# Where the copied sums of the second sweep's seven-product groups are added: in VectorE's accumulators, or by DMA in device memory

## The chip, the cores and the metric

The kernel runs on one core of a Trainium2 chip. The metric is the device time of one execution in microseconds (us), and the median of several runs is compared.

## What is computed

The reference takes attention over 32 memory slots per head, then a leaky two-layer network, then a bilinear one. The change touches the last of the three, and in it the last product alone:

```python
n_tokens, d_model, d_ff = (2304, 512, 1536)
...
def _moe2_ref(x, w_a, w_b, w_out) -> np.ndarray:
    a = x @ w_a
    b = x @ w_b
    return (a * b @ w_out).astype(np.float32)
```

## The kernel before

Activations stand with features on the 128 partitions and tokens along the columns; the result `out` lies in device memory as 128 partitions x 4 feature blocks x 2304 tokens. Every f32 operand is split into a high and a low part, and a product is three matrix passes of 512 columns each.

The bilinear stage runs in two **sweeps** over the hidden features (s = 0 and s = 1), each over half of the tokens; s = 1 is the last thing that the kernel does. A sweep takes the 1536 hidden features in 12 pieces of 128 (c = 0 to 11), two pieces forming a group q = 0 to 5. For each piece `ab_unit` (L1061) makes `a * b`, and for each group the product with `w_out` is added to the sweep's accumulators.

For q = 0 to 4 of the second sweep that last product is made in Strassen's manner, with seven products for a 2 x 2 split instead of eight: `o_part` issues one of them for a row half x (x = 0, 1), three passes at L1277. Four accumulators in SBUF, named `osum` and numbered d = 2, 3, 4, 7, hold the four quarters of the result. Products number 1, 6 and 7 are running sums in PSUM; ScalarE copies each to an SBUF tile `ok` (L1297). Products 2, 5 and 3 end a sum that VectorE adds from PSUM to `osum` 2, 7 and 3 (L1311, one SBUF and one PSUM input), and the copy `ok` belongs there too: in q = 0 VectorE makes `osum` of both at once (L1309), and in q = 1 to 4 it adds `ok` to `osum` by an instruction of its own (L1314, both inputs in SBUF). `osum` 4 has no copy to add.

The sixth group (q = 5) has eight plain products, made by `o_unit` (L1158, six passes each) at the very end, when nothing else is left for TensorE. VectorE adds each from PSUM to `osum` (L1171), and SyncE then issues the DMA of that part to `out` (L1179): twelve transfers, in the order in which the parts are finished. The last product is cut into a piece of 320 and one of 192 columns, so that the last addition and the last transfer are short.

The order of all instructions on each engine is written out by hand in two tables: `ORDER` lists the operations by number, with a letter for the engine where there is a choice, and `PLACES` gives every tile its room. SBUF tiles share 29 rooms named s0 to s28; a tile that takes over a room waits until the last reader of the tile before it is done. Each engine runs its own list in order, and an instruction that waits holds up all behind it on that engine.

Of the kernel before, what the change touches and what calls it, by code (L numbers as in the profile page):

```python
# [12 lines left out]
ALU = mybir.AluOpType  # L13
# [4 lines left out]
P = 128  # L18
# [10 lines left out]
NB2 = 512  # L29
# [55 lines left out]
def c_dma(nbytes):  # L85
    return max(0.6, nbytes / DMA_RATE)
# [7 lines left out]
305v 344 266a 168 103 141 267 268a 338 142 306a 127 345 269 337 143v 104 167 128 154 144 106 340 339a 145 155 342 108a 129 156 130 146v 158 131 343a 118 341
147 160a 119 364 121a 120a 132v 169 148a 105 86v 133 157 319 122 149v 318 134 153 260 320v 358 261a 123a 262 310 135v 263a 309 264 136 170 311v 124 151 172a
384 126v 137a 372 125a 138v 365a 107 312 159 390 179 109a 385 313 386 171 321 161a 391 110 314v 173a 373 322 359a 354 152 111a 323v 374 392 112 375v 348
113a 114v 315a 352 324a 316v 356 325v 355 349 387v 350 180 351v 393v 370 357v 298v 307v 181 360 97v 371a 353a 182 366 362 361 183 376 368 367 363v 184v 369v
185 174 377a 186 270 541 382 273a 271a 175a 272 187v 394 383a 274 188 176 532 346 178a 189a 177a 190v 395a 378 505 191 379 380 162 193 347a 192 194 275 550
195v 559 396 276a 278a 277 196 279 388 163a 197 542 414 381v 389a 198v 406 415 199 416 398 544v 200a 417v 164 201v 418 165a 166a 397 543 399v 545 407a 213
533 546 412 215 547v 214 548a 216 202 552 534 402 203 204 419a 217v 413a 408 561 205 403 280 409 206v 218 424 404 281a 405v 410 411v 432 425a 219 283a 436  # L100
434 207 282 208 285 437a 560 284 426 209v 433 288a 430 428 289 507 210 427 286a 211a 287 400 220v 431a 551 212v 420 221 442 429v 498 222a 535v 484 421 223v
491 422 423v 450 443a 435v 506 536 438 562v 451 537 452 444 401a 563 458 553v 446 453v 439 448 440 564 445 459 554 460 538v 441v 462 565v 447v 466 463 555
464 566a 454 556v 467 461v 472 468 455 456 478 557a 457v 567v 539a 470 499 549v 1274 492 1300 540v 1281 473 558v 479 449a 465v 474 469v 485 476 475v 486
508v 480 471a 481v 493 509 501v 500 494v 482 510 477a 1275 502 503 495 487v 496 572 483a 488 1276 489 1301 497v 1302 511v 490v 578 573a 504v 1277v 1303v 512
1278 579a 1304 1279 584 513a 515a 514 1305 590 1280v 516 1292a 1306v 585a 568 1293v 1307 1308a 1282 574 1310 1309v 1283 1284v 1314 522 569 1285 570 1286 575
580 576 1287v 591a 571v 586 581 1288v 1294a 577v 596 582 1289v 587 583v 588 1290v 1296a 1291v 589v 592 1298a 1297v 525a 598 593 1312 523a 602 1315 594 1322
595v 1341 1295v 1299v 604 524 1313 610 605 1311 526 606 608 597a 603 607v 517 609 614 520a 518a 521 1316 519 612 620 611 600 613v 599 601v 615 622 744 1318v
621 616 1319 624 623 626 617 1317 634 618 627 619v 630 1342 1320 628 625v 527 631 629v 632 1321v 644 765 633v 1333v 751 654 792 645 758 636 646 635 530a
528a 1343 529 638 1323 637v 1324 648 531 639 1334v 640 1344v 1351 1325v 647v 1345 641v 650 1326 649 656 651 652 662 653v 1346 660 801 663 1327 657 664 1328v
658 1347v 1335a 655 1348 1349a 668 1329v 746 1331v 1330v 642 1350v 1337a 1336v 1332v 753 661 745 1338v 752 674 665v 1353 759 1352 672 1339a 810 760 1355  # L110
1340v 643 1354 666 659v 675 670 676 669 677v 767 678 667 766 754v 671v 802 747v 793 761v 684 748 794 768v 679 804v 673 680 755 819 795v 690 682 762 811 796
685 681 803 769 813v 686 812 805 814 692 687 691 688 696 689v 694 693 749 756 770 702 820 683v 821 806 797 710 763 704 712 695v 1382 711 698 708 1356 699
700 1363 705 701v 706 697 822v 714 815 718 703 716 715 823 722 707v 719 717v 720 713v 726 723 721v 724 750v 730 727 757v 728 824 709 764v 771v 738 725v 798v
772 731 799a 729v 736 807v 816v 808a 800v 775a 740 825v 732 776 826a 809v 832 733 827v 773a 817a 774 739 734 741v 1357 818v 840 1358 735v 1364 1359v 828 833
1365 737 1384 834 1366v 1383 1360 742 842 1361 1362v 1385v 850 841 743 836 1374v 835 830 829 1367 856 851 837v 843v 1386 858 857 846 844 848 847 849v 831v
838 845 1368 864 839 782 852 783a 862 784 853 859 1369v 854 1375v 1376a 855v 860 777 1392 785a 1370v 1387 868 780a 863 1388v 778a 1371v 1389 1390v 870 1373v
874 786 871 865 866 861v 1378a 1372v 1391v 872 880 1380a 779 1396 1397 781 867v 876 1379v 873v 886 1394 877 1377v 878 1423 882 1381v 1404 890 881 1395 883
884 1393 787 885v 891 892 879v 887 869 888 894 1004 788a 889v 1011 893v 790a 898 875 1018 789 904 791 908 905 906 899 907v 900 895 1398 896 916 1405 897v
1400v 1399 1061 910 1401 1424 901v 1402 914 1025 1052 1403v 1407v 1415a 911 1416v 912 1406 1426v 902 1433 1408 918 913v 1425 1409 917 909 1427 1428 920
1429v 1410v 919v 915 928 1070 922 930 1431a 932 929 1432v 924 1006 903 1437 1013 1430 921 926 923 1411v 1005 1412v 1020 1414v 1413v 1417a 934 925v 1012  # L120
1419v 938 1026 931v 1019 1007v 935 936 944 1027 939 927 1053 937v 1054 1021v 962 1014v 1028v 933 1008 1009 940 1029 1071 952 1022 1015 1063 1055v 950 941
945 1062 1023 942 1064v 1072 1030 946 953 954 943v 958 1016 956 1073v 1079 960 1056 947 1065 959 1421a 1066 948 970 949v 951 964 955v 1074 974 1010v 965 966
968 971 963 975 961v 972 1017v 976 1031v 982 1057 969 986 984 1024v 978 957 973v 1032 1075 979 983 967v 980 998 988 981v 977v 1058v 992 1067v 990 1059v 993
999 1000 985v 994 1076v 1068a 1060v 1035a 1077a 996 991 1033a 987 1069v 1080 1036 1081 995v 1001v 1002 1078v 1420v 1034 1435 1438 1422v 1418v 1436 1092 997
1434 1445 1003 1464 989v 1082v 1083 1094 1084 1093 1088 1085v 1440 1042 1096 1095 1086a 1100 1439 1087v 1098 1043a 1089 1044 1090 1045a 1091v 1112 1101 1046
1102 1447 1110 1441v 1103v 1446 1097v 1442 1443 1106 1444v 1104 1108 1099 1107 1448v 1456a 1109v 1466 1111 1116 1457v 1113 1465 1449 1474 1114 1450 1122
1105 1467v 1115v 1451v 1118 1452v 1123 1124 1454v 1119 1453v 1120 1128 1458a 1117 1468 1126 1455v 1462a 1130 1125 1129 1121v 1176 1132 1127v 1460a 1037 1131
1461v 1528v 1476 1134 1038a 1040a 1039 1177 1041 1178 1047 1133v 1529v 1136 1459v 1135 1142 1137 1463v 1138 1146 1050a 1469 1477 1143 1150 1475 1144 1179v
1147 1145v 1148 1154 1470v 1139v 1472a 1140 1149v 1151 1051 1505 1152 1048a 1471 1155 1479 1049 1158 1156 1486 1153v 1141 1164 1160 1473v 1159 1162 1157v
# [164 lines left out]
def tile_mem_attention__leaky_mlp__bilinear_mlp(  # L294
# [842 lines left out]
    def o_unit(s, c, l, e, pos, cols=None):  # L1137
# [303 lines left out]
```

## Time and profile before

| | us |
|---|---|
| median of 3 runs | 778.22 |
| lowest, highest | 776.81, 778.3 |
| span of the profiled execution, from its first to its last instruction | 775.6 |
| TensorE busy in that span | 767.0 |
| VectorE busy | 647.7 |
| ScalarE busy | 402.6 |
| GpSimd busy | 0.7 |

The profiled execution is listed by its span. The median of the runs is 2.6 us longer than this span; that is what lies around it. TensorE's granted clock is 0.993 of its full level of 2.4 GHz over the span. GpSimd's 0.7 us all lie in the first two microseconds; it issues no DMA. All 59808 packets of the kernel's own data go through one queue, which SyncE feeds.

### The profile page before, as it was taken

Reading aid. Unit: us, or ns where it says so; the run is one execution under the profiler, and the core shown is the slowest. Engines: PE = TensorE matmul, PEld = TensorE weight load, DVE = VectorE, ACT = ScalarE, POOL = GpSimd, SP = SyncE. Lnnn points to the kernel's source line nnn. Section 1 sums busy time; section 2 is a strip of 40 time slices with the busy share of each in tenths; the row PEclk is TensorE's granted clock in tenths of the full one; section 3 lists DMA queues with packets and bytes.
Section 4 is the critical chain, followed back from the end, with each engine's and each line's share of the span. In section 5 each row is a group of like instructions: output and inputs, shape, how many; then the busy total and the mean of one; then the engine's idle time right before and its main releaser. Section 6 shows DMA issues by size and latency. Waiting matters only on the chain.

```text
span 775.6 us, 12742 instructions
## 1 busy us (share of the span) xinstructions
PE 767.0 (99%) x4766; PEld 656.8 (85%) x4766; DVE 647.7 (84%) x1249; ACT 402.6 (52%) x866; POOL 0.7 (0%) x6
## 2 busy tenths in 40 slices
PE   7999999999999999999999999999999999999998
PEld 6577898899889978898988888888888888888886
DVE  5897899689877989698685789999999688789877
ACT  5685786675546646654433445644543424444330
POOL 0000000000000000000000000000000000000000
PEclk9799999999999999999999999999999999999999
DMA  9993241665039141635973629775798685765523
GB/s 321 374 323 109 84 164 68 200 235 177 1 129 331 58 144 74 245 109 216 375 268 118 219 82 332 263 256 199 235 339 326 241 314 171 253 244 202 182 105 108
DMA packets 59868, 158.89 MB, mean 205 GB/s; under 512 B 7520, under 2 KB 22880, under 8 KB 59808
## 3 DMA queue, kind: packets, MB, share of 16 engines
q1 hardware_dynamic: 59808, 158.09, 57.6%
q8 instruction: 37, 0.61, 0.3%
q14 instruction: 23, 0.19, 0.1%
HBM read 111.41 MB, written 46.66 MB: 204 GB/s over the span
## 4 chain that ended last, share of the span: by engine, by line
PE 96%; DMA 2%; SPq 0%; DVE 0%; ACT 0%; issue 0%
PE y L840 24%; PE abx L1061 17%; PE h L788 13%; PE abz L1061 8%; PE o L1158 6%; PE os_x L1277 6%; PE aby L1061 4%; PE os_z L1277 3%; PE a L1115 2%; PE b L1115 2%; PE y L836 2%; PE vw L719 2%; PE os_y L1277 2%; DMA phi<-in_phiT_dram 1%; PE km L562 1%; DMA raw_win<-in_w_in_dram 1%
## 5 line engine op out<-in xcount | busy, mean ns | idle before, releaser
L840 PE MATMUL y<-g,wout 128*128 128x320 f32 (+2 forms) x1104 | 198.3, 333 | 0.0
L840 PEld LDWEIGHTS y<-g,wout 128*128 128x128 f32 x1104 | 175.0, 188 | 18.0 <-issue 3.8
L1061 PE MATMUL abx<-yb_T,wo 128*128 128x512 f32 x432 | 110.0, 390 | 0.0
L1061 PEld LDWEIGHTS abx<-yb_T,wo 128*128 128x128 f32 x432 | 80.1, 188 | 16.8 <-ACT t L1072 0.6
L1072 ACT COPY t<-abx 128x512 f32<-128x512 f32 x72 | 42.0, 586 | 61.7 <-PE abx L1061 60.6
L788 PE MATMUL h<-ahi,vwh 128*128 128x320 f32 (+1 forms) x240 | 72.8, 303 | 0.0
L788 PE MATMUL h<-ahi,vwl 128*128 128x320 f32 (+1 forms) x240 | 71.0, 296 | 0.0
L788 PE MATMUL h<-alo,vwh 128*128 128x320 f32 (+1 forms) x240 | 71.0, 296 | 0.0
L804 DVE TENSOR_TENSOR g<-t,g 128x256 fp32r<-128x256 f32 (+1 forms) x120 | 52.6, 452 | 15.9 <-ACT t L741 11.8
L741 ACT ACTIVATE g<-h 128x320 fp32r<-128x320 f32 (+1 forms) x120 | 48.3, 416 | 33.4 <-PE h L788 30.6
L741 ACT ACTIVATE t<-h 128x256 f32<-128x256 f32 (+1 forms) x120 | 49.4, 419 | 26.2 <-PE h L788 24.9
L1297 ACT COPY ok<-os_x 128x512 f32<-128x512 f32 x54 | 31.7, 586 | 58.9 <-PE os_x L1277 52.8
L788 PEld LDWEIGHTS h<-ahi,vwh 128*128 128x128 f32 x240 | 45.4, 189 | 8.0 <-issue 5.0
L859 DVE TENSOR_TENSOR acc<-y,acc 128x320 f32<-128x320 f32 (+1 forms) x72 | 39.3, 552 | 9.7 <-PE y L840 9.5
L788 PEld LDWEIGHTS h<-alo,vwh 128*128 128x128 f32 x240 | 45.5, 189 | 0.6
L788 PEld LDWEIGHTS h<-ahi,vwl 128*128 128x128 f32 x240 | 45.5, 190 | 0.0
L1069 DVE TENSOR_TENSOR t<-abz,t 128x512 f32<-128x512 f32 x48 | 32.9, 685 | 8.7 <-PE abz L1061 5.9
L1061 PE MATMUL abz<-yb_B,wo 128*128 128x512 f32 x144 | 36.7, 390 | 0.0
L1061 PE MATMUL abz<-yb_T,wo 128*128 128x512 f32 x144 | 36.6, 390 | 0.0
L1061 PE MATMUL abx<-yb_B,wo 128*128 128x512 f32 x144 | 36.5, 390 | 0.0
L1061 PE MATMUL aby<-yb_B,wo 128*128 128x512 f32 x144 | 36.5, 390 | 0.0
L1158 PE MATMUL o<-p,wout 128*128 128x512 f32 (+2 forms) x150 | 35.6, 383 | 0.0
(372 smaller groups left out, 1447.6 us busy)
## 6 DMA issues: line engine op xcount, KB each, us to landing
k_wo<-wo SPq DMA_DIRECT2D x24, 512.0 KB, 4.0
wo<-k_wo SPq DMA_DIRECT2D x24, 512.0 KB, 4.6
raw_wout<-in_w_out_dram SPq DMA_DIRECT2D x22, 512.0 KB, 5.4
raw_win<-in_w_in_dram SPq DMA_DIRECT2D x16, 512.0 KB, 6.6
kv<-in_kv_dram SPq DMA_DIRECT2D x16, 512.0 KB, 10.2
wf<-k_wf SPq DMA_DIRECT2D x9, 512.0 KB, 4.4
k_yb_T<-yb_T SPq DMA_DIRECT2D x8, 512.0 KB, 6.3
yb_T<-k_yb_T SPq DMA_DIRECT2D x8, 512.0 KB, 5.8
```

The lines of the kernel that those rows point to most:

```text
L741: nc.scalar.activation(dst, src, AF.Prelu, alpha=0.01)
L788: nc.tensor.matmul(T[o], T[w[u]][:, k, fs], T[a[v]][:, k, cols], start=(k == 0 and i == 0), stop=(k == 1 and i == 2))
L804: lambda T, e: engines[e].tensor_tensor(T[g][:, i, 1, to], T[t], T[g][:, i, 0, to].bitcast(F32), op=ALU.subtract),
L840: nc.tensor.matmul(T[o], w[:, u, here], T[g][:, j, v, at:at + m], start=(f == 0 and p == 0), stop=(f == 3 and p == 2))
L859: "DVE", c_dve(m), lambda T: nc.vector.tensor_tensor(T[acc][:, i, :], T[o], T[acc][:, i, :], op=ALU.add),
L1061: nc.tensor.matmul(T[o], T[w][:, which, u, k * P:(k + 1) * P], T[ys[v]][:, k, :], start=first and k == 0 and x == 0, stop=k == 1 and x == ...
L1069: op("DVE", 0.69, lambda T: nc.vector.tensor_tensor(T[to], T[o], T[x], op=ALU.add), r=[o, x], w=[to], tiles=[o, x, to])
L1072: op("ACT", 0.59, lambda T: nc.scalar.copy(T[t], T[X]), r=[X], w=[t], tiles=[X, t])
L1115: nc.tensor.matmul(T[o], T[w][:, k // 2, u, k % 2 * P:(k % 2 + 1) * P], T[ys[v]][:, k, :], start=(k == 0 and x == 0), stop=(k == 3 and x = ...
L1158: nc.tensor.matmul(T[o], T[w][:, u, es], T[g][:, at, v, here], start=(x == 0 and k == 0), stop=(x == 1 and k == 2))
L1277: nc.tensor.matmul(T[o], lhs(T, u), T[g][:, v, :], start=i in (1, 2, 5) and k == 0, stop=k == 2, skip_group_check=True)
L1297: op("ACT", 0.59, lambda T: nc.scalar.copy(T[k][:, x, :], T[o]), r=[o], w=[(k, x)], tiles=[o, k])
```

## The change

In the second sweep, for q = 1 to 4, VectorE's addition of `ok` to `osum` (L1314) goes away. In its place GpSimd issues DMAs from `ok` to the result in device memory: for q = 1 they write, for q = 2 to 4 they carry `accum_op` and add to what stands there. A copy of `osum` 2 is one transfer of 512 columns; one of `osum` 3 or 7 is two, of 320 and 192 columns. At the end the parts of `osum` 2, 3 and 7 can no longer overwrite `out`, so their DMAs move from SyncE to GpSimd and add as well; those of `osum` 4 stay on SyncE as they were. The first sweep is as before. The two tables are rewritten because the operations have new numbers.

```diff
@@ o_unit
+                d = acc[1] if s else 0
+                more = [("out", d, i, at)] if s and d != 4 else []
                 op(
-                    "DMA", c_dma(P * w * 4), lambda T, at=at, w=w, to=to: nc.sync.dma_start(out[:, e, to:to + w], T[acc][:, i, at:at + w]),
-                    r=[(ka, base) if cols else ka], tiles=[acc], ahead=1e12,
+                    "DMA", c_dma(P * w * 4),
+                    lambda T, at=at, w=w, to=to, more=more: (nc.gpsimd if more else nc.sync).dma_start(
+                        out[:, e, to:to + w], T[acc][:, i, at:at + w], **({"accum_op": ALU.add} if more else {})
+                    ),
+                    r=[(ka, base) if cols else ka], w=more, tiles=[acc], ahead=1e12,
                 )
@@ o_part
         if m:
-            op(
-                two(NB2), 0, lambda T, e: engines[e].tensor_tensor(into(T), into(T), T[k][:, x, :], op=ALU.add),
-                r=[(k, x)], w=[tok(d)], tiles=[k, acc(d)], ahead=1e12, soon=True,
-            )
+            hh, l = PART[d]
+            if s:
+                for at, w_, to in places_of(s, l):
+                    op(
+                        "DMA", 0,
+                        lambda T, at=at, w_=w_, to=to: nc.gpsimd.dma_start(
+                            out[:, 2 * hh + x, to:to + w_], T[k][:, x, at:at + w_], **({"accum_op": ALU.add} if q > 1 else {})
+                        ),
+                        r=[(k, x)], w=[("out", d, x, at)], tiles=[k], ahead=1e12, soon=True,
+                    )
+            else:
...
```

TensorE's and ScalarE's lists hold the same operations in the same order in both kernels. VectorE's list lacks 24 rows, SyncE's lacks 10, and GpSimd's has 50 more.

At the end of the kernel before, SyncE's list holds the transfers of the finished accumulators. In the names, `osum_3` is accumulator d = 3, `out_0_dram` is the result, and the brackets name the semaphores on which the instruction waits:

```order
L1179 DMA out_0_dram<-osum_3_7357 128x192 [waits DMAHW5_49,DVE_49]
L1179 DMA out_0_dram<-osum_3_7357 128x320 [waits DMAHW6_49]
L1179 DMA out_0_dram<-osum_2_7262 128x512 [waits DMAHW7_49]
L1179 DMA out_0_dram<-osum_3_7357 128x320 [waits DMAHW0_49,DVE_49]
L1179 DMA out_0_dram<-osum_3_7357 128x192 [waits DMAHW1_49]
L1179 DMA out_0_dram<-osum_7_7313 128x320 [waits DMAHW2_49,DVE_49]
L1179 DMA out_0_dram<-osum_7_7313 128x192 [waits DMAHW3_49]
L1179 DMA out_0_dram<-osum_7_7313 128x320 [waits DMAHW4_49,DVE_49]
L1179 DMA out_0_dram<-osum_7_7313 128x192 [waits DMAHW5_49,DVE_49]
```

The same nine transfers are GpSimd's last nine rows in the changed kernel:

```order
L1184 DMA out_0_dram<-osum_3_7357 128x192 [waits DMASW1_49,DVE_49]
L1184 DMA out_0_dram<-osum_3_7357 128x320 [waits DMASW2_49]
L1184 DMA out_0_dram<-osum_2_7262 128x512 [waits DMASW3_49]
L1184 DMA out_0_dram<-osum_3_7357 128x320 [waits DMASW5_49,DMASW4_49,DVE_49]
L1184 DMA out_0_dram<-osum_3_7357 128x192
L1184 DMA out_0_dram<-osum_7_7313 128x320 [waits DMASW6_49,DVE_49]
L1184 DMA out_0_dram<-osum_7_7313 128x192 [waits DMASW7_49]
L1184 DMA out_0_dram<-osum_7_7313 128x320 [waits DMASW0_49,DVE_49]
L1184 DMA out_0_dram<-osum_7_7313 128x192 [waits DMASW1_49,DVE_49]
```

All nine moved, in the same order, from SyncE's list to GpSimd's, behind the 40 transfers of `ok` and one more of `osum_2`. A wait for DMASW with a number is one for the eighth transfer before it on GpSimd's queue.

In the middle of the sweep, at the start of group q = 2, VectorE's list before reads so. Here `ok_1_1_1` is the copy of product 1 of group q = 1, `w2s_1_2` holds the sums of weights of group q = 2 and takes over a room, and `pT` and `pf` are sums of the hidden features:

```order
L1311 TENSOR_TENSOR osum_2_7262<-os_1_1_1_y_7590,osum_2_7262 128x512 [waits PE_49]
L1239 TENSOR_TENSOR pb_1_2_T2_7601<-pT_1_2_7495,pb_1_2_T2_7601 128x512 [waits Activation_49]
L1314 TENSOR_TENSOR osum_2_7262<-osum_2_7262,ok_1_1_1_7478 128x512 [waits DVE_49]
L1229 TENSOR_TENSOR pf_1_5_7542<-pf_1_5_7542,pT_1_2_7495 128x512
L1204 TENSOR_TENSOR w2s_1_2_7620<-wf_1_2_7530 128x256 [waits DMAHW4_49,DVE_49]
```

In the changed kernel it is:

```order
L1318 TENSOR_TENSOR osum_2_7262<-os_1_1_1_y_7593,osum_2_7262 128x512 [waits PE_49]
L1246 TENSOR_TENSOR pb_1_2_T2_7606<-pT_1_2_7498,pb_1_2_T2_7606 128x512 [waits Activation_49]
L1236 TENSOR_TENSOR pf_1_5_7545<-pf_1_5_7545,pT_1_2_7498 128x512
L1211 TENSOR_TENSOR w2s_1_2_7626<-wf_1_2_7533 128x256 [waits DMAHW4_49,DMASW5_49,DMASW0_49]
```

The addition of `ok_1_1_1` is gone, and the instruction that takes over that tile's room waits for GpSimd's transfers out of it instead of for VectorE.

## Rows read from the trace of the kernel before

**Rows 1.** The page: its span, and TensorE's busy time and instructions.
```profile
span 775.6 us, 12742 instructions
PE 767.0 (99%) x4766; PEld 656.8 (85%) x4766; DVE 647.7 (84%) x1249; ACT 402.6 (52%) x866; POOL 0.7 (0%) x6
```

**Rows 2.** Busy time of each engine by stretch, from the first L1314 group on.
```profile
core 0: us, PE busy (x) PEld busy (x) DVE busy (x) ACT busy (x) POOL busy (x), PEclk, DMA share, GB/s
660.00:685.00 25.00, 25.00 (x112) 20.67 (x112) 20.75 (x35) 12.31 (x22) 0.00 (x0) 1.00 0.61 206
685.00:710.00 25.00, 25.00 (x112) 20.71 (x111) 22.36 (x40) 10.22 (x18) 0.00 (x0) 1.00 0.58 213
710.00:735.00 25.00, 25.00 (x112) 20.71 (x111) 20.50 (x36) 9.49 (x18) 0.00 (x0) 1.00 0.68 250
735.00:760.00 25.00, 25.00 (x112) 20.70 (x111) 20.36 (x35) 8.23 (x15) 0.00 (x0) 1.00 0.23 85
760.00:776.00 16.00, 12.54 (x60) 10.34 (x58) 10.73 (x18) 0.62 (x1) 0.00 (x0) 0.98 0.37 131
```

**Rows 3.** The chain that ended last, its end: start, length, engine and line.
```profile
761.32 11.24 PE o L1158 x54
...
772.58 0.36 DVE osum L1171
```

**Rows 4.** VectorE's last instructions in time order: start us, length us, line, idle before.
```profile
768.15 0.69 DVE L1171 TENSOR_TENSOR osum<-o,osum 128x512 f32<-128x512 f32 x1
769.51 0.69 DVE L1171 TENSOR_TENSOR osum<-o,osum 128x512 f32<-128x512 f32 x1 [0.67 <-PE o L1158]
770.87 0.69 DVE L1171 TENSOR_TENSOR osum<-o,osum 128x512 f32<-128x512 f32 x1 [0.67 <-PE o L1158]
771.75 0.49 DVE L1171 TENSOR_TENSOR osum<-o,osum 128x320 f32<-128x320 f32 x1 [0.18 <-PE o L1158]
772.58 0.36 DVE L1171 TENSOR_TENSOR osum<-o,osum 128x192 f32<-128x192 f32 x1 [0.34 <-PE o L1158]
```

**Rows 5.** SyncE's issues at the end, merged and the last alone: start us, length us.
```profile
768.87 3.53 SPq L1179 DMA_DIRECT2D out_dram<-osum  x7
...
773.00 0.38 SPq L1179 DMA_DIRECT2D out_dram<-osum  x1
```

**Rows 6.** Line L1314 between 660 and 776: duration in ns, first and last start.
```profile
L1314 DVE TENSOR_TENSOR osum<-osum,ok x24: 681/684/687, 669.4 to 767.4; 128x512 f32<-128x512 f32 x24
```

**Rows 7.** Line L1179: how long SyncE needs for one issue, ns min/median/max.
```profile
L1179 SPq DMA_DIRECT2D out_dram<-oaccl x16: 332/432/936, 642.3 to 660.9; - x16
L1179 SPq DMA_DIRECT2D out_dram<-osum x12: 332/390/447, 763.4 to 773.0; - x12
```

**Rows 8.** DMA between 763 and 776: rate in 40 slices; issues, KB, us to landing.
```profile
GB/s 0 0 0 44 372 366 25 0 0 0 0 0 246 403 158 0 208 365 233 0 95 208 288 349 391 359 358 314 63 331 304 172 331 300 173 0 0 0 0 0
...
out_dram<-osum SPq DMA_DIRECT2D x4, 256.0 KB, 2.0
...
out_dram<-osum SPq DMA_DIRECT2D x4, 96.0 KB, 1.7
```

**Rows 9.** DMA issues between 660 and 760, the commonest load: KB, us to landing.
```profile
wo<-k_wo SPq DMA_DIRECT2D x21, 512.0 KB, 4.5
```

**Rows 10.** ScalarE's copy of a tile, and VectorE's first instruction in its room.
```profile
672.27 0.59 ACT L1297 COPY ok<-os_x 128x512 f32<-128x512 f32 x1 [1.77 <-PE os_x L1277]
...
678.09 0.42 DVE L1204 TENSOR_TENSOR w2s<-wf 128x256 f32<-128x256 f32 x1
```

More of the change, by code (lines that the diff above doesn't have):

```diff
@@ L94 @@
[L94 to L105, printed above, removed]
@@ L186 @@
[L186 to L188 removed]
+24 246 0 4 238 1 26 25 224 27 3 28 2 247 29 31 30 231 248 249v 34a 250 32a 251 35 33 45 239 240 241v 23 252v 242 253 5 44 243 6 244v 22 36 7 8 46 226 37
@@ new lines @@
+1850v 2024 1858v 1936 1930 2119 2047 2064 1928 1970 1932a 2026 1977v 2039 2025 1994 1999 1971v 2145 1931v 2126 1978a 1972v 2046 2028 1974v 1934a 1973v
+1938a 1975v 2027 2018 1980a 1935v 2040 1981v 2006 1979v 1996 1916 1933v 1982a 2030 1939 2000 1983v 1940a 2008 1997 2065 2002 1995 1941v 2066 2041v 2020a
+2029 2001 2003 2042 2043 2031 2032 2048v 2049 2004 2050 2067v 2044v 2034 2005 2033 2056a 2120 2057v 2009 2121 2051v 2074 2068 2058a 2036 2069 2146 2007
+2147 2086 2035 2128 2010 2127 2059v 2011 2037 2070v 2100 2148v 2071 2072a 2149 2075 2014a 2012 2079 2073v 2015v 2078 2019 2013v 2150 2102 2052v 2053v 2054v
@@ new lines @@
+2151v 2217 2095 2060a 2152 2153a 2061v 2080 2094 2103 2076 2016a 2224 2055v 2101 2062a 2082 2017v 2096a 2063v 2021 2081 2154v 2022a 2083 2088 2106 2023v
+2243 2122v 2084 2325 2129v 2123 2077 2107 2159 2130 2104 2124 2085 2110 2105 2131 2089 2125v 2087 2137a 2108 2132v 2219 2091 2138v 2139a 2109 2218 2155
+2097 2299 2112 2225 2090 2092 2114a 2226 2167 2113 2098a 2111 2133v 2181 2099v 2134v 2093v 2183 2140v 2135v 2156 2136v 2182 2160 2141a 2143a 2142v 2227v
+2185 2157 2161 2220v 2184 2144v 2162 2228 2158 2245 2186 2244 2163 2221 2300 2222 2229 2189 2223v 2230v 2235a 2187 2169 2164 2326 2236v 2327 2165 2231v
@@ new lines @@
+2253 2188 2190 2191 2166 2232v 2233v 2301 2234v 2237a 2168 2170 2239a 2328v 2240v 2193 2246v 2255 2247 2192 2172 2248 2194 2258 2241a 2173 2171 2176 2242v
+2210a 2115v 2256 2302v 2175 2174v 2306 2329 2249v 2281 2177a 2303 2250 2215a 2330 2273 2259 2331v 2251a 2304 2332 2333a 2279 2414 2178 2260 2334v 2305v
+2282 2317a 2261 2280 2179a 2238v 2275a 2318v 2254 2285 2262 2116v 2283 2252v 2263 2211v 2307 2195 2335 2284 2204v 2401 2265 2400 2286 2205a 2257 2309v
+2117a 2180v 2339 2347 2310 2308 2206v 2264 2311 2340 2266 2312v 2270 2267 2319a 2313v 2341 2314v 2355 2196v 2321a 2207v 2197v 2315v 2268 2404 2322v 2316v
@@ new lines @@
+2320v 2287 2271 2274 2288 2198v 2323a 2199v 2269 2405 2208a 2289 2402 2276 2200a 2342 2290 2324v 2371 2212v 2415 2201v 2343 2372 2209v 2294a 2376 2407
+2202a 2292 2203v 2377 2356 2118v 2403 2293 2416 2213a 2272v 2409 2291v 2344 2434 2406 2357a 2214v 2361 2435 2216v 2345 2277a 2295v 2362 2349 2436 2278v
+2296v 2346 2363 2437 2297a 2350 2408 2348 2364 2352 2358 2298v 2359a 2351 2373 2417 2353 2410 2365 2374 2412 2419 2413 2366 2354v 2368 2367v 2398a 2421
+2393v 2420 2369 2438 2394v 2422 2387v 2360v 2439 2444 2423 2440v 2388a 2441 2445 2378 2389v 2424 2375v 2442 2411 2446 2425 2466 2395v 2426 2337 2447 2396a
@@ new lines @@
+2467 2399v 2524 2427 2338 2450 2390v 2448 2443v 2431 2468 2451 2370v 2526 2428 2391a 2488 2449 2429 2397v 2392v 2489 2471 2469 2432 2379v 2486 2381v 2472
+2433v 2509 2487 2380v 2478 2430 2525 2383a 2336 2461a 2384v 2510 2473 2591 2462v 2527 2382v 2480 2385a 2474 2490v 2386v 2491 2492 2475 2463v 2529 2493
+2464a 2465v 2476 2530 2548 2477 2494 2479 2549 2481 2495 2483 2482 2517a 2531 2592 2518v 2496 2532 2497 2484 2498 2499 2485v 2533 2550 2511v 2522a 2534
+2500 2551 2512a 2514v 2501v 2552 2535 2519v 2504 2515a 2503 2502 2553 2520a 2536 2505 2554 2537 2544 2506v 2555 2538 2507 2539 2508 2556 2418 2545 2470
@@ L222 @@
+b7 b1 b2 t1 t4 t0 g1 b3 g7 b4 g4 f7 b4 b4 s12 g6 f0 s10 s22 s10 s18 g3 f1 g0 b0 b6 b5 t2 t3 t1 s6 b3 b3 b4 s3 b3 f1 s13 s23 f1 g3 s2 g1 s4 s13 s11 s9 s11
+b1 b2 b7 t0 t4 t2 s9 f7 g4 b3 b4 b3 f0 g6 s17 s20 s12 s8 f4 g7 s4 s22 b1 b5 b0 t1 t3 t0 s16 b3 b4 s8 b3 f4 g4 s9 s2 s8 g0 f7 s4 g7 s3 s10 s13 s7 s10 b2 b7
+b5 t2 t3 t1 s7 b3 b4 b3 s11 g1 s9 s2 f0 s18 s6 g3 s3 s12 b0 b7 b1 t4 t0 t2 f1 s7 b3 b4 g6 b3 s18 s16 s17 s13 s23 s20 s6 b5 b7 b1 t1 t2 t3 s25 s17 b3 b4 b3
+b3 b4 b3 b4 b3 b4 b3 b4 b3 b4
 """
@@ L1312, in o_part @@
         if m:
-            op(
-                two(NB2), 0, lambda T, e: engines[e].tensor_tensor(into(T), into(T), T[k][:, x, :], op=ALU.add),
-                r=[(k, x)], w=[tok(d)], tiles=[k, acc(d)], ahead=1e12, soon=True,
-            )
+            hh, l = PART[d]
[9 more added lines that the diff above has]
+            else:
+                op(
+                    two(NB2), 0, lambda T, e: engines[e].tensor_tensor(into(T), into(T), T[k][:, x, :], op=ALU.add),
+                    r=[(k, x)], w=[tok(d)], tiles=[k, acc(d)], ahead=1e12, soon=True,
+                )
         if 2 * q + 2 == NC2:
```

223 lines of the change are left out of this document (106 added, 117 removed).

## The prediction

> **What bounds the kernel now.** I read the page first: TensorE is busy for 767.0 of 775.6 us [rows 1]. A busy share of 99% can still hide stalls, so the next view was the table by stretch, over the part that the change touches. In all four stretches from 660 to 760 TensorE is busy for 25.00 of 25.00 us at full clock, while VectorE is busy for 20 to 22 us of each [rows 2]. The reader is to see that TensorE has no gap there that a freer VectorE could close. TensorE's list of operations is the same before and after, so the middle of the sweep can only stay as long as it is or grow.
>
> The other place is the end. The chain that ended last runs through the 54 matrix passes of the plain products from 761.32 on, and then through VectorE's short last addition [rows 3]. That addition ends at 772.58 + 0.36 = 772.94 [rows 4], SyncE issues the last transfer at 773.00 [rows 5], and the span ends at 775.6 [rows 1]. So 2.6 us lie behind the last addition, and nothing covers them: whatever makes this tail longer makes the kernel longer by the same amount.
>
> The profiled execution has a span of 775.6 us, and the median of the runs is 2.6 us above it. I make the sum against the span and add the difference to the median of 778.22.
>
> **What is removed.** 24 additions at 0.684 us [rows 6], 16.4 us of VectorE's time. Between 660 and 760 no TensorE work waits on VectorE [rows 2], so I cost this at nothing. At the end it is nothing again: between the last additions VectorE already sits idle for 0.67, 0.67, 0.18 and 0.34 us, each time waiting for TensorE [rows 4], so the last one cannot start earlier. Value: 0.
>
> **What one of GpSimd's transfers costs.** The trace of before has no DMA issued by GpSimd, so two prices are bounded by the nearest rows. The first is T, the time for which GpSimd is held by one issue. From below it is SyncE's median, 0.39 us [rows 7]. From above I take 1.6 us, a whole transfer from issue to landing rounded below the shortest median of 1.7 [rows 8], as if GpSimd were held until its data is away. I take the longest issue that SyncE shows, 0.94 us [rows 7], because GpSimd writes the work list of 128 rows by program, and this is the nearest row for a slow issue.
>
> The second price is the time to landing of a transfer that adds. From below it is that of a plain store of the same size, 1.7 us for 96 KB [rows 8]. From above it is this plus a whole load in front, 1.7 + 4.5 = 6.2 us [rows 9], since the old value must come out of device memory before the sum goes back. I take a read as short as the write without its issue, 1.7 - 0.39 = 1.3 us, so 3.0 us from an issue as short as SyncE's, and 3.0 + (0.94 - 0.39) = 3.55 us from the start of GpSimd's.
>
> **The 40 transfers in the middle of the sweep.** They are ten per group over some 100 us; 40 x 0.94 = 38 us of an engine that does nothing else. What could hurt is a room that comes free later: nine instructions on VectorE, ScalarE and SyncE that take over a room of an `ok` tile now wait for a transfer. The tightest that I found is the sum of weights for q = 2. The `ok` tile is complete at 672.27 + 0.59 = 672.86, and VectorE begins in its room at 678.09 [rows 10], or 0.6 us earlier without the addition that stood ahead of it in the list. The cover is 678.09 - 0.6 - 672.86 = 4.6 us. A transfer of 256 KB lands 2.0 us after its issue when plain [rows 8]; with the longer issue that is 2.55, and this group of q = 1 only writes. So it fits with 2 us to spare. If it did not, what is queued behind it on VectorE is the rest of that sum and the additions from PSUM, and TensorE would be late only after VectorE's 20.75 busy us of 25 [rows 2] are used up. Value: 0; with T at 1.6 us and a landing as late as a load's 4.5 us [rows 9], 6.1 us in all, VectorE would wait 1.5 us, which its idle share still takes.
>
> The transfers also share the DMA engines with the loads of weights, at a DMA share of 0.58 to 0.68 up to 735 [rows 2]. 6.3 MB come on top in 100 us, 63 GB/s beside some 200. Value: 0, with 2 us as the upper end.
>
> **The tail.** Nine transfers that SyncE issued go to GpSimd, in the same order. Their data are ready at the ends of VectorE's last five additions, 768.84, 770.20, 771.56, 772.24 and 772.94 [rows 4], and three of them hang on the first of these. SyncE itself was close to its limit: seven issues fill 3.53 us from 768.87 on [rows 5], 0.50 us each with what lies between them. GpSimd at 0.94 us each is slower than the data arrive: nine in 772.94 - 768.84 = 4.1 us, one per 0.46 us. So it is held without a break, and the wait for VectorE's last addition is replaced by a wait for GpSimd's own queue. It starts at 768.87; the ninth issue starts at 768.87 + 8 x 0.94 = 776.39, lands 3.55 us later at 779.94, and the end follows as it did behind SyncE's last transfer, 775.6 - (773.00 + 1.7) = 0.9 us, at 780.84. Against 775.6 that is **+5.2 us**, the whole of the sum. Predicted time: 778.22 + 5.2 = 783.4 us. The lower end of the prices (0.39 us and 1.7 us) gives 773.00 + 1.7 + 0.9 = 775.6, that is +0. The upper end (1.6 us and 6.2 us) gives 768.87 + 12.8 + 6.2 + 1.2 + 0.9 = 789.97, that is +14.4 us or 792.6.
>
> The Trainium skill speaks against a queue here: "DMA: Bandwidth & Descriptors", section "Anatomy of one DMA — SWDGE (gpsimd) path", puts a GpSimd-issued DMA at about 2.0 us fixed plus its bytes at 436 GB/s, calls most of this the receipt of the last byte, and calls the writing of the descriptors small. By it, as an estimate, the last 96 KB would land 2.2 us after their data, against the 1.7 us of SyncE's row, and the kernel would take about 778.7 us. No row of before can decide between that and a held GpSimd.
>
> **Rivals.** *GpSimd issues as fast as SyncE, so no queue forms.* The last transfer then starts at 773.00 as before and lands between 0 and 1.3 us later than it did: 778.2 to 779.5 us, not measurably slower. It decides where T is below (772.94 - 768.84) / 8 = 0.51 us. For it speaks that SyncE does it in 0.39 [rows 7], and the skill's small descriptor cost named above has this result; against it, that the nine transfers that go together are many and even SyncE fell to 0.50.
>
> *The transfers themselves are the queue.* The nine carry 1.31 MB. Plain stores there run at up to 300 to 400 GB/s [rows 8]. If adding costs two reads and a write and the engines do it at a third, 120 GB/s, the data alone need 10.9 us from 769.8 on, and with 1.3 and 0.9 us behind them the end is at 782.9: +7.3, or 785.5 us. If the same slowness makes the reuse of rooms late in mid-sweep, 2 to 6 us come on top, so 785 to 792. It decides from about 140 GB/s down, where 1.31 MB take longer than nine issues (8.5 us). For it speaks that each byte crosses the engines more often; against it, that the DMA engines are idle ahead of 763 [rows 2, 8].
>
> *The freed VectorE lets TensorE run faster.* There is no idle TensorE time from 660 to 760 to win [rows 2], so at most the 0.2 to 0.3 us around the last additions: 778.0. It decides only if stalls hide in TensorE's busy time.
>
> That the change does not take place can be left out: the built order shows 50 transfers on GpSimd's list and 24 additions fewer on VectorE's.
>
> **How the numbers follow.** Forecast, a queue on GpSimd at the end: 0.69, from 779.8 to 789. Transfers as the queue: 0.20. No queue: 0.09. A gain: 0.02. The predicted time is that of the forecast, 783.4. The range leaves out the no-queue case below 779.5 and the highest end of the slow transfers above 791, together less than 0.2. A measurement of this kernel can tell about 0.2% or 1.6 us from no change. Faster by more than that: 0.02 or less; within it: the no-queue case, 0.09; slower: the forecast and the slow transfers, 0.89.
>
> **What would show it.** In the profile of the changed kernel the rows of GpSimd's issues at the end should follow each other without a gap, each near 0.94 us, the last starting some 3 us after VectorE's last addition. TensorE should still be busy for 25.00 of 25 us from 660 to 760 and end near 772.5. A landing near 3 us for the small transfers bears out the second price. The prediction is wrong if GpSimd's last issue starts within 0.1 us of VectorE's end (no queue), if the issues are done early and the landings are long (the transfers are the queue), or if TensorE ends later than 773 (the rooms or the loads came late).

## The result, and the profile after

| | before | after |
|---|---|---|
| median, us | 777.65 (4 runs, 776.81 to 778.3) | 785.56 (4 runs, 784.3 to 787.65) |
| after / before | | 1.0101, 95% interval 1.008 to 1.0122 |
| span of the profiled execution, us | 775.6 | 782.9 |

The change makes the kernel 1% slower. The median of before is over the three runs shown ahead and one more beside the runs of after. The prediction said 783.4 us, between 779.5 and 791.0, with a chance of 0.89 for slower: right in sign, in place and nearly in size. In the medians the loss is 7.9 us and in the spans 7.3, where its sum had 5.2.

The page of the changed kernel answers to [rows 1]: the span, the busy times, and the packets of SyncE's and GpSimd's queues. VectorE lost its 24 additions, and GpSimd now feeds a queue of its own.

```profile
span 782.9 us, 12788 instructions
PE 766.4 (98%) x4766; PEld 656.5 (84%) x4766; DVE 634.9 (81%) x1225; ACT 402.8 (51%) x866; POOL 41.3 (5%) x56
q1 hardware_dynamic: 58368, 156.52, 56.8%
q0 software_dynamic: 6304, 7.87, 6.4%
```

Busy time by stretch, as in [rows 2]:

```profile
core 0: us, PE busy (x) PEld busy (x) DVE busy (x) ACT busy (x) POOL busy (x), PEclk, DMA share, GB/s
660.00:685.00 25.00, 25.00 (x112) 20.71 (x111) 18.46 (x31) 12.30 (x22) 6.15 (x11) 1.00 0.77 272
685.00:710.00 25.00, 25.00 (x112) 20.71 (x111) 19.98 (x34) 10.06 (x18) 8.16 (x10) 1.00 1.03 279
710.00:735.00 25.00, 25.00 (x112) 20.68 (x111) 17.50 (x30) 9.48 (x17) 8.74 (x10) 1.00 1.03 300
735.00:760.00 25.00, 25.00 (x112) 20.71 (x111) 17.24 (x28) 8.13 (x14) 8.74 (x10) 1.00 0.76 148
```

TensorE is busy for the whole of every stretch, as before. VectorE is 2 to 3 us less busy in each, and nothing comes of it. The share of the DMA engines went from 0.58 and 0.68 to 1.03 between 685 and 735, so they are full there, and still no TensorE work waits.

The end of the program, from the timeline of VectorE and of GpSimd (start us, length us, instruction, in brackets the idle time ahead), and the tail of the chain that ended last:

```profile
768.83 7.99 POOL L1184 DMA_DIRECT2D out_dram<-osum  x9 [4.57 <-DVE osum L1173]
772.26 0.36 DVE L1173 TENSOR_TENSOR osum<-o,osum 128x192 f32<-128x192 f32 x1 [0.33 <-PE o L1160]
```
```profile
761.00 11.23 PE o L1160 x54
772.63 3.29 POOL out_dram L1184
775.92 0.89 POOLq L1454
```

VectorE's last addition ends at 772.62, against 772.94 in [rows 4]: all work on the data is done as early as before. The chain as the view shows it ends with GpSimd's last issue at 776.81; what fills the 6.1 us from there to the end is in the next two views. From 768.83 on GpSimd issues nine transfers without a gap, 7.99 / 9 = 0.89 us each, until 776.82. SyncE needed until 773.38 for them [rows 5].

The DMA view from 769 to 783 shows what the issues do not: 40 slices of 0.35 us (the busy share of the engines in tenths, and the rate), then GpSimd's queue (packets, MB, share) and its issues (count, KB, median us to landing). Behind them, for the same nine transfers, stand the issue records with ns min/median/max and first and last start, and for the last of them the spread of the times to landing.

```profile
DMA  0008699959998999999999999999940000000000
GB/s 0 0 0 33 44 165 98 59 80 198 184 117 146 168 174 170 143 157 186 119 179 179 170 152 124 151 155 181 152 57 7 0 0 0 0 0 0 0 0 0
q0 software_dynamic: 1296, 1.31, 72.5%
out_dram<-osum POOLq DMA_DIRECT2D x4, 160.0 KB, 6.1
out_dram<-osum POOLq DMA_DIRECT2D x4, 96.0 KB, 6.1
out_dram<-osum POOLq DMA_DIRECT2D x1, 256.0 KB, 5.6
```
```profile
L1184 POOL DMA_DIRECT2D out_dram<-osum x9: 862/2266/3646, 768.8 to 773.2; - x9
DMA to landing us min/median/max: 5.9/6.4/6.9
```

The engines are full from 770.2 to 779.7, about 9.5 us for 1.31 MB, or 138 GB/s. In [rows 8] the same bytes, written only, went at 300 to 400 GB/s in most slices and were away by 774.3. With the DMA view narrowed to slices of 25 ns, the last packet of after is at 779.70 and the last of before at 774.32.

The times to landing have to be read with care. An issue's record opens while GpSimd still works on the issues ahead: the ninth opens at 773.2 and lasts 3.6 us, but its turn comes at 776.82 - 0.89 = 775.93. It lands 6.9 us after it opens, near 780.1, which is 4.1 us from its turn.

One more row belongs to the end. GpSimd closes the program with DRAIN instructions. These are their rows in the two kernels, after first (count, then ns min/median/max, first and last start):

```profile
L1454 POOLq DRAIN  x3: 40/102/9226, 772.9 to 782.7; - x3
```
```profile
L1436 POOLq DRAIN  x3: 34/78/386, 1.0 to 775.4; - x3
```

In after one drain lasts from 772.9, beneath the last issues, to 782.1, which is 2.4 us past the last packet, and the span ends 0.8 us behind it. In before the longest takes 386 ns, at the start of the program. So the 7.3 us split in two: the last packet is 779.70 - 774.32 = **5.4 us** later, and the end follows it after 3.2 us instead of 1.3, **1.9 us** more. The experiments ask what sets each part.

### The profile page after: what moved, and what is told of

It is laid out like the page before. It is cut to its first block, busy times and chain, and to the rows that moved or that the text cites. A ratio compares the mean times of both kernels' runs of the same rounds, so it can differ in the third digit from the quotient of the medians.

```text
span 782.9 us, 12788 instructions
## 1 busy us (share of the span) xinstructions
PE 766.4 (98%) x4766; PEld 656.5 (84%) x4766; DVE 634.9 (81%) x1225; ACT 402.8 (51%) x866; POOL 41.3 (5%) x56
## 3 DMA queue, kind: packets, MB, share of 16 engines
q0 software_dynamic: 6304, 7.87, 6.4%
## 4 chain that ended last, share of the span: by engine, by line
PE 95%; DMA 2%; SPq 0%; POOL 0%; DVE 0%; POOLq 0%; ACT 0%; issue 0%
PE y L842 24%; PE abx L1063 17%; PE h L790 13%; PE abz L1063 8%; PE o L1160 6%; PE os_x L1284 6%; PE aby L1063 4%; PE os_z L1284 3%; PE a L1117 2%; PE b L1117 2%; PE y L838 2%; PE vw L721 2%; PE os_y L1284 2%; DMA phi<-in_phiT_dram 1%; PE km L564 1%; DMA raw_win<-in_w_in_dram 1%
## 5 line engine op out<-in xcount | busy, mean ns | idle before, releaser
L1325 POOL DMA_DIRECT2D out_dram<-ok x40 | 31.8, 886 | 725.8 <-ACT ok L1304 725.8
```

The costliest lines, as they stand in the source:

```text
L1325: lambda T, at=at, w_=w_, to=to: nc.gpsimd.dma_start(out[:, 2 * hh + x, to:to + w_], T[k][:, x, at:at + w_], **({"accum_op": ALU.add} if q ...
```

## The experiments

All times below are ratios to the kernel before on the same chip, with 95% intervals, unless only a span is given. The profiled executions reach their tail at times that differ by up to 2 us, so tails are compared from the first issue of the tail on.

### The middle and the end, each alone

**mid_only** is after with all final transfers back on SyncE and writing.

```diff
-lambda T, at=at, w=w, to=to, more=more: (nc.gpsimd if more else nc.sync).dma_start(
-    out[:, e, to:to + w], T[acc][:, i, at:at + w], **({"accum_op": ALU.add} if more else {})
+lambda T, at=at, w=w, to=to, more=more: nc.sync.dma_start(
+    out[:, e, to:to + w], T[acc][:, i, at:at + w]
```

> The 40 transfers of the copies in mid-sweep stay on GpSimd as in the changed kernel; at the end all twelve parts go out from SyncE as plain writes, as before the change (so the copied sums are overwritten and missing from the result). All theories that put the loss at the end: TensorE full from 660 to 760, span 775.3 to 775.8 us, ratio to before 1.000 within 0.002. Theory that the mid-sweep transfers cost time (rooms or loads late): span 777 us or more. Theory that any use of GpSimd's queue costs a fixed time at the program's end (its closing drain): span 777.6 us with nothing lost earlier.

Measured: 1.0007 (0.9993 to 1.0021). The stretches from 685 to 735 are as full as those of after, with the DMA engines at a share of 1.00 and 1.02:

```profile
span 776.6 us, 12795 instructions
685.00:710.00 25.00, 25.00 (x112) 20.72 (x111) 19.82 (x34) 10.06 (x19) 8.75 (x10) 1.00 1.00 271
710.00:735.00 25.00, 25.00 (x112) 20.72 (x111) 17.78 (x31) 8.79 (x17) 8.74 (x10) 1.00 1.02 302
```

The span is 0.8 us above the expected 775.8, but short of the 777.6 of a fixed closing time. Most of the 0.8 lies elsewhere: between 400 and 500, long ahead of the change, TensorE is busy for 99.37 of 100 us in this execution and for 100.00 in before. So 40 transfers and the loss of 24 additions together cost and gain nothing that can be measured over the ten runs.

**tail_only** is before with the end of after: the copies of q = 1 are written out by GpSimd as the values to add to, and VectorE keeps the additions of q = 2 to 4. At the end its edit is that of the change.

```diff
...
@@ o_part, from before
+if s and q == 1:
+    op(two(NB2), 0, lambda T, e: send(T), r=[(k, x)], w=[tok(d)], tiles=[k, acc(d)], ahead=1e12, soon=True)
+else:
     op(
         two(NB2), 0, lambda T, e: engines[e].tensor_tensor(into(T), into(T), T[k][:, x, :], op=ALU.add),
...
```

> VectorE makes the additions of groups q = 2 to 4 as before the change; only q = 1 is sent by GpSimd (as plain writes, so that there is something to add to), and the end is that of the changed kernel: ten parts added by GpSimd's DMAs. Loss at the end (all three accounts of it: issues, transfers, drain): span near the changed kernel's 782.9 us, +7 us. Loss in mid-sweep: span below 778 us.

Measured: 1.0079 (1.0058 to 1.0101), span 783.0. The loss is at the end: the interval overlaps that of after, 1.008 to 1.0122. The row of GpSimd's issues that answers to that of after:

```profile
770.03 7.96 POOL L1181 DMA_DIRECT2D out_dram<-osum  x9 [4.55 <-DVE osum L1171]
```

Its last packet is at 781.00, 10.97 us after the first of these issues; in after it is 10.87.

### What holds the last byte: issues, bytes, or adding

**tail_plain** is after, with the nine transfers on GpSimd but only writing.

```diff
-out[:, e, to:to + w], T[acc][:, i, at:at + w], **({"accum_op": ALU.add} if more else {})
+out[:, e, to:to + w], T[acc][:, i, at:at + w]
```

> As the changed kernel, but GpSimd's ten transfers at the end write instead of adding (the copied sums are overwritten and missing). Issue account: a plain write is issued in 0.54 us as in q = 1, the ninth starts at 773.2 and lands some 2 us later, span 776 to 776.5 us. Transfer account: plain writes run at some 300 GB/s, same span; the whole loss of 7 us belongs to the adding. If GpSimd's way of sending is slow in itself, adding or not: 780 us or more. If the closing drain adds its 2 us whenever GpSimd's transfers are still under way at the end: 778 us.

Measured: 1.0032 (1.0019 to 1.0046). GpSimd's issues, and two rows of the DMA view from 762 to 785, which holds 1.57 MB of GpSimd's, the nine transfers and one more of `osum` 2; behind them, on its own, the row of after in the same view:

```profile
span 778.5 us, 12788 instructions
768.72 4.85 POOL L1184 DMA_DIRECT2D out_dram<-osum  x9 [4.88 <-DVE osum L1173]
q0 software_dynamic: 544, 1.57, 19.3%
out_dram<-osum POOLq DMA_DIRECT2D x4, 96.0 KB, 2.2
```
```profile
q0 software_dynamic: 1440, 1.57, 53.3%
```

Nine issues take 4.85 us, 0.54 us each, so issuing an addition takes longer than issuing a write. At 0.54 us GpSimd nearly keeps up with the data: the last packet is at 774.77, only 0.45 us later than in before. The same bytes occupy the DMA engines for 19.3% of 23 us when written, 4.4 us, and for 53.3% when added, 12.3 us: adding costs 2.8 times as much engine time. In the spans adding is 782.9 - 778.5 = 4.4 us of the 7.3. Of the 2.9 us that remain, 0.45 are in the transfers. The other 2.4 lie behind them: the end follows the last packet after 3.7 us instead of 1.3, and 3.0 of these pass before GpSimd's drain ends. The span is nearest to the 778 expected if the drain adds to the end.

**merged** is after with each pair of 320 and 192 columns of one part sent as a single adding transfer of 512, where the part is finished at once: six issues at the end instead of nine, the same bytes.

```diff
+whole_row = bool(more) and l == 1 and not cols
+if whole_row:
+    w, to = (0, to) if at else (NB2, (2 * s + 1) * S)
...
```

> As the changed kernel, but at the end the pieces of 320 and 192 columns go as one transfer of 512 except for the very last part: six issues instead of nine behind the first, the same 1.31 MB (the tokens of those parts land in another order in the result). Issue account: no queue of issues is left, the last issue starts right behind VectorE's last addition near 772.7 and lands 3.5 us later, span near 779 us. Transfer account: the DMA engines are full either way, the last byte stays near 779.8, span 782 to 783 us.

Measured: 1.0079 (1.0053 to 1.0106).

```profile
span 782.0 us, 12787 instructions
768.64 5.33 POOL L1187 DMA_DIRECT2D out_dram<-osum  x6 [4.58 <-DVE osum L1173]
q0 software_dynamic: 1008, 1.57, 48.9%
out_dram<-osum POOLq DMA_DIRECT2D x5, 256.0 KB, 6.1
```

The third row is again that of the DMA view from 762 to 785. Counted from the first issue of the tail, the issues end 5.33 us on instead of 7.99, but the last packet, at 778.90, comes 10.26 us on instead of 10.87, only 0.6 us earlier. If the queue of issues held the last byte, most of the 2.66 us would have come back. They did not. What fell as little as the last packet is the engines' time, from 53.3% to 48.9% of 23 us, 1.0 us: the adding transfers themselves hold the end. The last of the six has its turn at 773.97 - 0.89 = 773.08 and lands near 779.2, 6.1 us later, where the ninth of after took 4.1.

**tail_half** is after with each adding transfer of the end carrying half its columns. It was run once, so it has no ratio.

```diff
-out[:, e, to:to + w], T[acc][:, i, at:at + w], ...
+out[:, e, to:to + (w // 2 if more else w)], T[acc][:, i, at:at + (w // 2 if more else w)], ...
```

> As the changed kernel, but the ten adding transfers at the end carry half the columns each (the other half of those columns lacks its last part): as many issues and as many rows, half the bytes. Issue account: the last issue still ends near 776.8 and its transfer 1 to 1.5 us later, last packet near 778.2, span near 781.4 us. Transfer account, paid by bytes: the engines need some 5 us for 0.66 MB and are no longer full, so the issues bind and the last packet is again near 778.2. Transfer account, paid by rows: the engines stay full and the last packet stays at 779 or later, span 782 us or more.

The tail's issues, and GpSimd's queue from 769 to 783, as shown for after (1.31 MB, 72.5%):

```profile
span 782.7 us, 12788 instructions
769.82 7.98 POOL L1184 DMA_DIRECT2D out_dram<-osum  x9 [4.58 <-DVE osum L1173]
q0 software_dynamic: 1296, 0.66, 53.7%
```

The issues take 7.98 us as in after, so an issue's time does not depend on the columns. The engines' time falls by 18.8% of 14 us, 2.6 us: halving the bytes takes off a quarter of it, not a half, so adding has a large share that does not go by the byte. (Some rows of the halved transfers are only 384 bytes long; no run tells whether rows so short cost more for themselves.) The last packet comes 9.37 us after the first issue, where after needed 10.87, so only 1.5 of the 2.6 us show. It comes 1.4 us after the last issue ends, where the single adding transfer of last_add below needs 1.6, so the issues are now what it waits for, though the engines are still busy for 7.5 of these 9.4 us. The expected numbers by rows (last packet at 779 or later, span 782 or more) came too, but by the late start of this tail: counted from the first issue, 9.37 us is what the issues alone were expected to give, 778.2 - 768.83. So the queue of issues is the next limit, about 1.5 us below the engines' own. The span did not follow, since this execution began its tail 1 us later than after's and its drain ended 2.7 us behind the last packet.

### Fewer accumulators

**only_first** and **first_two** are before with the change made for accumulator 2 alone, or for 2 and 3, whose parts are finished first; the others are added by VectorE and written by SyncE.

```diff
+more = s and acc[1] in (2,)        # first_two: (2, 3)
...
+if s and d == 2:                   # first_two: d in (2, 3)
+    op(two(NB2), 0, lambda T, e: send(T), r=[(k, x)], w=[tok(d)], tiles=[k, acc(d)], ahead=1e12, soon=True)
+else:
```

> Only accumulator 2, the one that is finished first at the end, takes the changed way: its copies go by GpSimd's DMAs (8 transfers in mid-sweep), its two parts are added by GpSimd at 763.4 and 764.8; accumulators 3 and 7 are as before the change. Transfer account and drain account: GpSimd's transfers and its closing drain are over by 770 to 771, span 775.3 to 776 us, ratio to before 1.000 within 0.002. If adding DMAs cost something wherever they stand, or the drain costs its 2 to 3 us whenever GpSimd has sent anything: 777.5 us or more.

> Accumulators 2 and 3 take the changed way, 7 is as before. Five adding transfers with 0.79 MB are left behind 768.8. Transfer account with the drain: at some 140 GB/s the last byte moves near 775.5, the end follows about 3 us later, span 778 to 779 us. Issue account without a drain: the fifth issue starts at 772.4 and lands 3.5 us later, span 776.8 us.

Measured: only_first 1.0006 (0.9996 to 1.0016), first_two 1.0067 (1.0054 to 1.008). GpSimd's tail and closing drain of only_first, then of first_two:

```profile
765.47 0.86 POOL L1181 DMA_DIRECT2D out_dram<-osum  x1 [0.50 <-DVE osum L1171]
L1451 POOLq DRAIN  x3: 39/102/5723, 765.5 to 776.0; - x3
```
```profile
span 780.4 us, 12769 instructions
769.24 4.42 POOL L1181 DMA_DIRECT2D out_dram<-osum  x5 [2.79 <-DVE osum L1171]
L1451 POOLq DRAIN  x3: 40/93/8613, 771.0 to 780.1; - x3
```

In only_first the drain ends at 771.2 beneath TensorE's work, and the kernel takes the time of before. In first_two I expected the last byte at 775.5, and GpSimd's came at 778.0 (SyncE's near 778.2): five adding transfers share the engines with SyncE's stores of the other accumulators, which I had left out. The two queues from 768 to 779, GpSimd's first:

```profile
q0 software_dynamic: 904, 0.93, 60.6%
q1 hardware_dynamic: 854, 1.03, 28.3%
```

No kernel of this study was faster than before; only_first is the form of the change that equals it and keeps the whole result.

### The closing drain

tail_plain left two accounts. Either GpSimd's drain takes a fixed time of some 4 us from its last issue, or it takes time for each transfer that GpSimd has issued. **last_plain** and **last_add** are before with two of GpSimd's transfers in the whole program: 192 columns of one copy in q = 1, written, and the very last 192 columns of the result. In last_plain the last one writes, in last_add it adds.

```diff
+last = s and cols and at
...
+nc.gpsimd.dma_start(out[:, e, to:to + w], T[acc][:, i, at:at + w])      # last_add: accum_op=ALU.add
+if last else nc.sync.dma_start(out[:, e, to:to + w], T[acc][:, i, at:at + w])
...
```

> As before the change, but the very last transfer of 192 columns goes from GpSimd, as a plain write (so 192 columns lack one copied sum, which is sent and then overwritten). Drain account: the issue takes 0.54 us from 773.0, the closing drain ends some 4 us behind it, and the end 0.8 us later: span 778.3 to 778.6 us, +2.8 us for one transfer. If the drain only mirrors many transfers under way: span 775.8 to 776.2 us.

> As the run with the last transfer from GpSimd, but that transfer adds to the copied sum sent in mid-sweep. Transfer account with the drain: one adding transfer of 96 KB has the engines for itself and hides under the drain, span 778.5 to 779 us, at most 0.5 us above the plain one. Issue account with a fixed landing near 6 us for an adding transfer: 780 us or more.

Measured: last_plain 1.0012 (1.0002 to 1.0022), last_add 1.0018 (1.0009 to 1.0027). Issue, landing and drain of each:

```profile
span 776.4 us, 12745 instructions
773.42 0.54 POOL L1182 DMA_DIRECT2D out_dram<-osum  x1 [93.96 <-DVE osum L1171]
out_dram<-osum POOLq DMA_DIRECT2D x1, 96.0 KB, 1.9
L1447 POOLq DRAIN  x3: 34/93/2077, 773.4 to 776.1; - x3
```
```profile
span 776.5 us, 12745 instructions
772.54 0.87 POOL L1182 DMA_DIRECT2D out_dram<-osum  x1 [93.92 <-DVE osum L1171]
out_dram<-osum POOLq DMA_DIRECT2D x1, 96.0 KB, 2.9
L1447 POOLq DRAIN  x3: 34/93/3047, 772.5 to 776.2; - x3
```

Both spans came out some 2 us below what the fixed drain wanted, so that account falls. The drains end only 0.5 us behind the last packets, and SyncE's own first closing DRAIN in before starts as late, at 774.9 after a last packet at 774.32. These two runs also price a single transfer of 96 KB on idle engines: 1.9 us when it writes and 2.9 us when it adds, against SyncE's 1.7 [rows 8].

**mid_split** is after with each of the 40 transfers of mid-sweep issued as two of half the columns: 90 transfers in the program instead of 50, the same bytes, the same tail.

```diff
-lambda T, at=at, w_=w_, to=to: nc.gpsimd.dma_start(
-    out[:, 2 * hh + x, to:to + w_], T[k][:, x, at:at + w_], ...
+lambda T, at=at, w_=w_, to=to: [
+    nc.gpsimd.dma_start(
+        out[:, 2 * hh + x, to + j:to + j + w_ // 2], T[k][:, x, at + j:at + j + w_ // 2], ...
+    ) for j in (0, w_ // 2)
+],
```

> As the changed kernel, but each of the 40 transfers of copies in mid-sweep goes as two halves, so GpSimd sends 90 transfers in all instead of 50; the ten at the end are the same. Theory that the closing drain is paid per transfer that the program sent from GpSimd (so far about 0.5 us plus 0.04 us each, from runs with 2 to 50 of them): the drain ends some 3.9 us behind the last packet instead of 2.4, span 784 to 785 us, 1.5 us over the changed kernel. Rival, the drain only mirrors the transfers still under way at the end: 2.4 us as in the changed kernel, span 782.5 to 783.3 us. If the mid-sweep transfers are not hidden after all, TensorE shows waits between 660 and 760.

Measured: 1.0123 (1.0102 to 1.0144). TensorE is busy for 24.84 of 25 us in the stretch from 710 to 735 and without a gap in the other three, so at most 0.16 us are lost there; the span also holds a tail that begins 1.7 us later than that of after.

```profile
span 786.6 us, 12838 instructions
770.54 7.99 POOL L1184 DMA_DIRECT2D out_dram<-osum  x9 [4.58 <-DVE osum L1173]
L1456 POOLq DRAIN  x3: 40/102/11137, 774.7 to 786.3; - x3
```

The last packet is at 781.68, 11.14 us after the first issue of the tail (after: 10.87). The drain ends at 774.7 + 11.14 = 785.8, which is 4.2 us behind it. The account by transfers said 3.9, the other 2.4. Transfers issued up to 100 us earlier, and long landed, make the end later. All kernels by the number of transfers that GpSimd issued in the program:

| kernel | transfers | GpSimd's last packet, us | drain ends, us | between |
|---|---|---|---|---|
| last_plain | 2 | 774.95 | 775.5 | 0.5 |
| last_add | 2 | 775.05 | 775.6 | 0.5 |
| only_first | 10 | 770.35 | 771.2 | 0.9 |
| tail_only | 20 | 781.00 | 782.2 | 1.2 |
| first_two | 30 | 778.00 | 779.6 | 1.6 |
| mid_only | 40 | 762.36 | 764.4 | 2.1 |
| merged | 47 | 778.90 | 781.2 | 2.3 |
| after | 50 | 779.70 | 782.1 | 2.4 |
| tail_half | 50 | 779.19 | 781.9 | 2.7 |
| tail_plain | 50 | 774.77 | 777.7 | 3.0 |
| mid_split | 90 | 781.68 | 785.8 | 4.2 |

Most lie within 0.1 us of 0.5 us + 0.04 us per transfer; tail_half and tail_plain lie 0.2 and 0.5 us above it. It is not the number of packets: tail_plain has 5408 on GpSimd's queue, after 6304, and the longer time behind them. All of these transfers have 128 rows, so whether the price is one per transfer or per row is not shown. What GpSimd does in that time no row shows either. Of the kernels with 30 transfers or more, the two above the line are those whose last packet follows soonest behind the end of GpSimd's last issue: after 1.2 us (tail_plain) and 1.4 us (tail_half), and after 2.2 to 4.9 us in the others. In both the drain ends some 4.1 us behind that issue. Part of its work may therefore run beneath the last transfers; that is a reading, and no run tests it.

## Why the prediction was right, and where its sum was off

- **The middle of the sweep, 0 us: right.** mid_only shows it by itself. The cover named for it held: VectorE's waits between 660 and 760 end with TensorE or ScalarE, none with a transfer, though the transfers land after 3.8 to 5.9 us in the median. The doubt about the loads was well placed but needless: the commonest load takes 5.2 us instead of 4.5 [rows 9], and TensorE waits for none.
- **The place of the loss, the end behind VectorE's last addition: right.** tail_only loses most of it, mid_only nothing.
- **GpSimd held for 0.94 us by one issue: nearly right.** It is 0.89 for an addition and 0.54 for a write. Held without a break, and issues ending some 4 us after VectorE: as forecast.
- **A landing at 3.55 us from the start of the issue: near in size; that the sum came out with it was luck.** On idle engines it is 2.9 us (last_add); for the ninth of after it is 4.1 us from its turn on GpSimd. The forecast's last landing of 779.94 agrees with the measured one near 780.1, but the sum came to it by the wrong binder: the ninth issue, then one landing. merged shows that fewer issues bring back 0.6 us of 2.66. What ends last is the nine transfers going through full engines. That is the mechanism of the rival called *the transfers themselves are the queue*, to which the text gave 0.20, with adding at a third of a write's rate and 120 GB/s; measured are 1/2.8 and 138. The text put the point where this rival decides at about 140 GB/s; by its own 8.5 us for nine issues it is 1.31 MB / 8.5 us = 154 GB/s. The measured rate lies below both, yet near, so forecast and rival end close together, and tail_half shows the queue of issues 1.5 us behind as the next limit. By the signs that the text named, the issues came as in the forecast and the landings came late as in the rival. The reason held against the rival, idle DMA engines ahead of 763, was no argument: they were idle for want of work.
- **The end 0.9 us behind the last landing, as behind SyncE: the step that failed.** It was taken over from [rows 5] and [rows 8], where GpSimd issues nothing. With 50 transfers its closing drain ends 2.4 us behind the last packet and the span 0.8 us after that. In the sum's own terms: the ninth issue has its turn at 775.93 (forecast 776.39), lands 4.1 us later (3.55), and the end follows 2.8 us behind that (0.9). This last term is 1.9 us more than in before, and it is most of the gap between the 7.3 us of the spans and the 5.2 of the sum.
- **The 2.6 us between span and median: not all of it lies around the span.** In every execution for which both are on record the time is 1.7 to 2.2 us above the span, 1.8 in the median. So the profiled execution of before was some 0.8 us quicker than the median of 778.22 to which the sum was added, and the median of four runs, 777.65, lies lower too.
- **The rival without a queue: half right.** For writes GpSimd does issue almost fast enough (tail_plain, 0.54 us, against the limit of 0.51 that the text gave), and the data are late by 0.45 us only. It failed on the adding and on the drain. The rival of a freed VectorE fell as expected: 12.8 us less of VectorE's busy time gave nothing. (The sum's 16.4 us are the lengths of the 24 additions; an addition can begin before the instruction ahead of it has ended, the last of them at 767.40 against 766.79 + 0.69 = 767.48, so less busy time goes.)

A plain transfer of 96 KB from GpSimd lands after 1.9 to 2.2 us here. The Trainium skill, "DMA: Bandwidth & Descriptors", section "Anatomy of one DMA — SWDGE (gpsimd) path", gives 2.0 us and the bytes at 436 GB/s, which is an estimated 2.2 us for 96 KB; the rows agree. It does not hold for a transfer that adds, which takes 2.9 us alone and 4.1 us as the last of nine. The section calls the generation of descriptors small. No row here shows that part alone, but a whole issue holds GpSimd for 0.54 us when it writes and 0.89 when it adds, one after the other.

## What to carry to other kernels

Work taken off an engine that has slack gained nothing here, and what takes its place has to be priced where it ends, not where the work was. The adding DMAs were free only while other work covered them, down to their drain: in only_first both ended beneath TensorE's work, and SyncE wrote the last parts. When GpSimd gets a program's first DMAs, look for its closing drain in a trace; the transfer of the last byte is not the end.

## What the runs showed of the hardware beyond what was expected

- An adding transfer of 128 rows holds GpSimd for 0.86 to 0.89 us, with 96 columns (tail_half) as with 512 (merged); a writing one holds it for 0.54 to 0.57.
- Adding takes 2.8 times the engine time of writing for the same bytes (53.3% against 19.3%). Of it a quarter goes when the bytes are halved. The number of packets does not explain it: GpSimd's ten written transfers go in 544 packets and ten adding ones in 1440, but SyncE's twelve writes in before have 144 each as well and cost as little per MB as GpSimd's written ones (25.7% for 2.10 MB, against 19.3% for 1.57), and merged, with 1008, saves little.
- GpSimd's drain ends later behind the last packet by about 0.04 us for each transfer of 128 rows that it issued anywhere in the program: 0.5 us with 2, 4.2 us with 90.
